# Layer 2 of the 448-token slots with the weights stationary, and the way back of its rows through DRAM

## The chip, the core and the metric

The kernel runs on one core of a Trainium2 chip. The time is the device time of one execution in microseconds (us). The five engines of the core that matter here are TensorE (PE; PEld is its weight load), VectorE (DVE), ScalarE (ACT), GpSimd (POOL) and SyncE (SP), which issues most of the DMAs. Every engine works through its own instructions in order.

## The reference

The tokens pass through an attention with sigmoid weights; then each of the 3584 tokens goes to one of eight experts, whose two layers are a matmul, a ReLU and a matmul.

```
x = attn_out.transpose(0, 2, 1, 3).reshape(3584, 768)
e_idx = np.argmax(x @ w_gate, axis=1)
gate_w = softmax(x @ w_gate)[e_idx]
eom = 1.0 / (1.0 + np.exp(-(x @ w_output_gate)))
for e in range(8):
    mask = e_idx == e
    h = np.maximum(x[mask] @ w1[e], 0.0)      # 768 -> 1024
    ye = h @ w2[e]                            # 1024 -> 768
    out[mask] = gate_w[mask, None] * eom[mask, e, None] * ye
```

## The kernel before

The first part is the attention, which also writes x to DRAM (`x_dram`) and routes the tokens: for each expert a list of its tokens' rows. The second part works in slots. A slot is up to 448 tokens of one expert (a 448-token slot, `TB`) or up to 240 (a half slot, `TM`). With these inputs nine slots run: seven of 448 tokens and then two half slots. The first four 448-token slots always run; those after them and the half slots stand in branches.

All matmuls of a slot are done as three, because each operand is split into a high part and a low part (`split`: ACT copies the rounded high part, DVE subtracts to get the low part): high times high, low times high, high times low.

Layer 1 of a slot has eight groups f of 128 hidden units. A group is 6 x 3 matmuls (L458 to L460) with w1 stationary and the tokens moving, 448 or 240 columns. ACT then writes the ReLU's high part (L471, `hh`) and DVE its low part (L472, `hl`; for a 448-token slot in two pieces, 384 and 64 columns, since the low part of the last 64 tokens lies next to their high part in `hr`).

Layer 2 before has the tokens stationary: for 128 tokens t and one half n of the 768 outputs, 8 x 3 matmuls (L486 to L488) of 384 columns, with the token block as the weights and w2 moving. A 448-token slot has three such blocks and 64 tokens over. Those go through `layer2_rest` (L530, L531): a stationary block of which 64 rows are the high and 64 the low part of the same tokens, 2 x 16 matmuls of 384 columns more. ACT evicts each PSUM tile with the token's weight as scale (L492), and GpSimd scatters the 128 rows to `out` with an indirect DMA (L515). The last PSUM tile of a 448-token slot is kept (`left`) and evicted and scattered in the next slot (`finish`, L506). In a half slot the last 128 rows are scattered in two halves of the columns.

Around the matmuls a slot prepares the next one (`slot`). In layer 1 GpSimd gathers the next slot's x rows (L384, 14 gathers for 448 tokens, 8 for a half slot), w2 of this slot is split in pairs of rows (f = 1 to 4), and SP loads the next w1 in three parts behind it (`w1r` and `w2r` lie in the same memory). After layer 1 DVE transposes the gathered rows (`turn_x`, L428); they are split (`split_x`) and w1 is split (`split_w1`) during layer 2, and SP loads the next w2 in four parts behind that. Layer 2 uses three PSUM banks in turn (`psy`), layer 1 three others (`psh`). The order on each engine is the order in which the code is written (`manual_schedule`). L385 to L397 issue the weight loads; L661 is the attention's store of x, four DMAs of 32 x 14 runs of 192 numbers each.

Of the kernel before, what the change touches and what calls it, by code (L numbers as in the profile page):

```python
# [8 lines left out]
F32 = mybir.dt.float32  # L9
# [12 lines left out]
E = 8  # L22
# [33 lines left out]
class Kernel:  # L56
# [19 lines left out]
    def memory(self):  # L76
        self.rounded = self.pool("rounded").tile([128, ROUNDED // 4], F32R, name="rounded")
        self.plain = self.pool("plain").tile([128, PLAIN // 4], F32, name="plain")
        ps = self.pool("psum", space=PSUM).tile([128, 8, 512], F32, name="ps")
        self.ps_s = [ps[:, 0:2], ps[:, 2:4]]  # L80
        self.ps_o = [[ps[:, 4], ps[:, 5]], [ps[:, 6], ps[:, 7]]]
        self.ps_s2 = ps[:, 6:8]
        self.psh = [ps[:, i] for i in (0, 1, 2)]
        self.psy = [ps[:, i] for i in (4, 5, 3)]
        self.ps_step = [ps[:, i, 0:8] for i in (7, 3)]
        self.rot = {}
        self.beat = [None, None]
        self.hints = {2: [ET.Activation, ET.DVE, ET.Pool], 5: [ET.PE]}

        c = self.carve  # L90
        w = c(0, 3, 2, 2, DF)
        self.w1s = [[w[:, d // 2, a, d % 2] for d in range(6)] for a in range(2)]
        self.w1p = [[w[:, k, a] for k in range(3)] for a in range(2)]
        self.xs = [c(12 * DF * 4 + i * 6 * TB * 4, 6, TB) for i in range(2)]

        self.w1r = c(0, 6, DF, dt=F32)
        self.w2r = c(0, 8, DM, dt=F32)
        self.xg = c(6 * DF * 4, GB_, Q4, dt=F32)
        self.xT = c(6 * DF * 4 + XG, 6, TB, dt=F32)
# [27 lines left out]
    def constants(self):  # L127
# [3 lines left out]
        self.x_dram = dram.tile([NT, DM], F32, name="x_dram")  # L131
        self.lst = dram.tile([E * CAP, W], I32, name="lst")
# [29 lines left out]
        self.halves = cp.tile([128, 3], I32, name="halves")  # L162
        self.left, self.left_at = None, cp.tile([128, 1], I32, name="leftat")
        self.left_w = cp.tile([128, 1], F32, name="leftw")
# [299 lines left out]
    def layer1(self, f, n, begun=False):  # L464
        nc = self.nc
        if not begun:
            self.layer1_mm(f, n)
        ps, r = self.h_ps, n % 128 if n == TB else 0
        m = n - r
        hh, hl, hr = self.hs[0][:, f, 0:n], self.hs[1][:, f, 0:m], self.hr[:, f, r:]  # L470
        self.beat[0] = nc.scalar.activation(hh, ps, AF.Relu).ins  # L471
        lo = lambda out, a, b: nc.vector.scalar_tensor_tensor(  # L472
            out, ps[:, a:b], 0.0, r32(hh[:, a:b]), ALU.max, ALU.subtract)
        lo(hl, 0, m)
        if r:
            lo(hr, m, n)

    def layer2(self, s, t, n, y, last=0):
# [10 lines left out]
        if last == TB and n == 1:  # L489
            self.left = ps  # L490
# [19 lines left out]
    def half_rows(self, at):  # L510
        for n in range(2):
            self.nc.vector.tensor_scalar(self.halves[:, n:n + 1], at, 2.0, float(n), ALU.mult, ALU.add)
# [7 lines left out]
    def layer2_rest(self, s):  # L520
        nc = self.nc
        lt, y = s["lt"], self.ys[1]
        lo, hi = slice(0, 64), slice(64, 128)
        for n in range(2):
            c = slice(384 * n, 384 * n + 384)
            ps = self.take("y", self.psy)[:, 0:384]
            for f in range(8):
                h = self.hr[:, f]
                wh, wl = self.w2_at(f, c)
                nc.tensor.matmul(ps, h, wh, start=(f == 0), stop=False)  # L530
                nc.tensor.matmul(ps, h, wl, start=False, stop=(f == 7))  # L531
            nc.scalar.activation(y[lo, c], ps[hi], AF.Copy, scale=r32(lt[hi, 3, 1:2]))
            nc.vector.scalar_tensor_tensor(y[lo, c], ps[lo], r32(lt[lo, 3, 1:2]), y[lo, c], ALU.mult, ALU.add)
        self.scatter(lt[lo, 3, 0:1], y[lo])

    def slot(self, cur, nxt, side=None, begun=False, hint=None):
# [5 lines left out]
        self.finish()  # L542
        self.rot["y"] = 1
        for f in range(8):
# [20 lines left out]
        ws = {0: (0, 1), 1: (2,)} if n == TB else {0: (0,), 1: (1, 2)}  # L565
        xs = {2: (0,), 3: (1, 2)} if n == TB else {0: (0,), 1: (1,), 2: (2,)}
        for i in range(2 * (n // 128)):
            t = i // 2
            if hint is not None and i in self.hints:
                hinted = self.hints[i]  # L570
                more = self.nc.values_load(self.more[0:1, hint[1]:hint[1] + 1], engines=hinted, min_val=0, max_val=1)
                self.tc.mark_branch_hint_location(hint[0], hint=more, engines=hinted)
            self.layer2(cur, t, i % 2, self.ys[(t + (t > 0 and n % 128 > 0)) % 2], n if t == n // 128 - 1 else 0)
            if nx is not None:
# [4 lines left out]
                for k in xs.get(i, ()):  # L579
                    self.split_x(nx, k)  # L580
            if i == 3 and n == TB:
                self.nc.vector.tensor_copy(self.left_at, cur["lt"][:, 2, 0:1])
                self.nc.vector.tensor_copy(self.left_w, r32(cur["lt"][:, 2, 1:2]))
            if i == 0 and n < TB:
                self.half_rows(cur["lt"][:, 1, 0:1])
            if side is not None:
                next(side, None)
            if i == 1 and n % 128:
                self.layer2_rest(cur)
        return nx  # L590

# [189 lines left out]
    def build(self, phases="abc"):  # L781
# [64 lines left out]
        with tc.manual_schedule():  # L846
            self.finish()
        mid = lambda k: lambda: (self.slot_regs(self.tab_b, k, self.ltb[:, k], self.lxb[:, k], False), NT, False)
        lists = lambda k: dict(lt=self.ltb[:, k], lx=self.lxb[:, k])
        with ExitStack() as ctx:  # L850
            for k in range(E):
                ctx.enter_context(tc.If(part > k))
                with tc.manual_schedule():
                    self.slot(lists(k), mid(k + 1) if k + 1 < E else None)
# [35 lines left out]
```

## Time and profile before

| | |
|---|---|
| median of three runs | 763.12 us (762.82 to 763.97) |
| the profiled execution | 765.36 us |
| its span, first to last instruction | 763.6 us |
| PE busy | 754.4 us, 99% of the span |
| granted TensorE clock | 0.998 |
| DMA | 126.53 MB, mean 166 GB/s |

The profile is of one execution. Times in its rows count from the start of the span. A matmul's row has the time from its start to the end of its pipeline, and the next matmul starts before that; so the pace of PE is read from the distance of the starts. What ended an engine's idle time before an instruction stands behind it as "<-".

### The profile page before, as it was taken

Reading aid. Unit: us, or ns where it says so; the run is one execution under the profiler, and the core shown is the slowest. Engines: PE = TensorE matmul, PEld = TensorE weight load, DVE = VectorE, ACT = ScalarE, POOL = GpSimd, SP = SyncE. Lnnn points to the kernel's source line nnn. Section 1 sums busy time; section 2 is a strip of 40 time slices with the busy share of each in tenths; the row PEclk is TensorE's granted clock in tenths of the full one; section 3 lists DMA queues with packets and bytes.
Section 4 is the critical chain, followed back from the end, with each engine's and each line's share of the span. In section 5 each row is a group of like instructions: output and inputs, shape, how many; then the busy total and the mean of one; then the engine's idle time right before and its main releaser. Section 6 shows DMA issues by size and latency. Waiting matters only on the chain. (4 is left out here: it accounts for less than half of the span.)

```text
span 763.6 us, 14912 instructions
## 1 busy us (share of the span) xinstructions
PE 754.4 (99%) x5817; PEld 580.2 (76%) x5817; DVE 397.9 (52%) x731; ACT 372.0 (49%) x429; POOL 270.7 (35%) x379
## 2 busy tenths in 40 slices
PE   9999999999999999999999999999999999999996
PEld 4444444444344379999999999999999999999996
DVE  1364746556687759524615625615524534454554
ACT  5666666666677632523433424424424433344544
POOL 5002102020444437288237137227217216324142
PEclk9999999999999999999999999999999999999999
DMA  8465665746796646626526425334344352463641
GB/s 302 145 179 145 196 154 162 211 130 172 253 291 194 165 117 207 200 65 210 182 83 221 141 109 194 118 155 160 123 172 127 134 215 85 175 220 111 221 144 41
DMA packets 73721, 126.53 MB, mean 166 GB/s; under 512 B 15442, under 2 KB 53484, under 8 KB 73632
## 3 DMA queue, kind: packets, MB, share of 16 engines
q1 hardware_dynamic: 62784, 99.95, 42.4%
q0 software_dynamic: 9776, 24.53, 9.4%
q10 hardware_dynamic: 1072, 0.92, 0.5%
q8 instruction: 50, 0.82, 0.5%
q14 instruction: 39, 0.32, 0.1%
HBM read 108.77 MB, written 23.09 MB: 173 GB/s over the span
## 5 line engine op out<-in xcount | busy, mean ns | idle before, releaser
L635 ACT ACTIVATE a<-ps,bias_s 128x896 f32<-128x896 f32 x168 | 168.7, 1007 | 86.9 <-PE ps L633 83.6
L384 POOL DMA_INDIRECT plain<-x_dram,lxs x112 | 139.3, 1244 | 76.0 <-ACT h L471 25.2
L633 PE MATMUL ps<-q,k 64*64 64x448 f32 x1344 | 157.9, 541 | 1.2 <-ACT a L635 0.8
L642 PE MATMUL ps<-a,v 64*64 64x448 f32 x1344 | 156.3, 536 | 0.0
L458 PE MATMUL ps<-rounded 128*128 128x448 f32 (+1 forms) x432 | 149.9, 347 | 0.8 <-ACT y L506 0.8
L460 PE MATMUL ps<-rounded 128*128 128x448 f32 (+1 forms) x432 | 149.1, 345 | 0.0
L459 PE MATMUL ps<-rounded 128*128 128x448 f32 (+1 forms) x432 | 149.1, 345 | 0.0
L410 DVE TENSOR_TENSOR rounded<-plain,rounded 128x2048 fp32r<-128x2048 f32 (+5 forms) x63 | 96.8, 1573 | 71.8 <-ACT rounded L409 71.8
L486 PE MATMUL ps<-w2h,h 128*128 128x384 f32 x400 | 133.7, 334 | 0.0
L488 PE MATMUL ps<-w2h,h 128*128 128x384 f32 x400 | 133.7, 334 | 0.0
L487 PE MATMUL ps<-w2l,h 128*128 128x384 f32 x400 | 133.7, 334 | 0.0
L472 DVE SCALAR_TENSOR_TENSOR h<-ps,h 128x384 fp32r<-128x384 f32 (+2 forms) x128 | 44.9, 387 | 139.8 <-ACT h L471 136.7
L471 ACT ACTIVATE h<-ps 128x448 fp32r<-128x448 f32 (+1 forms) x72 | 36.5, 507 | 155.4 <-PE ps L460 148.9
L633 PEld LDWEIGHTS ps<-q,k 64*64 64x64 f32 x1344 | 50.9, 134 | 76.5 <-issue 69.4
L642 PEld LDWEIGHTS ps<-a,v 64*64 64x64 f32 x1344 | 51.6, 133 | 74.7 <-issue 71.3
L458 PEld LDWEIGHTS ps<-rounded 128*128 128x128 f32 x432 | 81.2, 188 | 6.7 <-ACT y L506 1.1
L460 PEld LDWEIGHTS ps<-rounded 128*128 128x128 f32 x432 | 81.2, 188 | 5.0
L459 PEld LDWEIGHTS ps<-rounded 128*128 128x128 f32 x432 | 81.2, 188 | 4.9
L409 ACT CAST rounded<-plain 128x2048 fp32r<-128x2048 f32 (+5 forms) x63 | 81.8, 1331 | 0.6 <-DVE plain L434 0.6
L515 POOL DMA_INDIRECT out<-y,lts x21 | 30.9, 1470 | 136.2 <-ACT y L492 73.3
L487 PEld LDWEIGHTS ps<-w2l,h 128*128 128x128 f32 x400 | 75.1, 188 | 0.1
L486 PEld LDWEIGHTS ps<-w2h,h 128*128 128x128 f32 x400 | 75.1, 188 | 0.1
(146 smaller groups left out, 685.6 us busy)
## 6 DMA issues: line engine op xcount, KB each, us to landing
plain<-w SPq DMA_DIRECT2D x40, 768.0 KB
plain<-w SPq DMA_DIRECT2D x27, 1024.0 KB
k<-kT SPq DMA_DIRECT2D x23, 448.0 KB
q<-qT SPq DMA_DIRECT2D x23, 448.0 KB
x_dram<-xt SPq DMA_DIRECT2D x30, 336.0 KB
v<-vm SPq DMA_DIRECT2D x23, 384.0 KB
plain<-w SPq DMA_DIRECT2D x6, 512.0 KB
plain<-x_dram,lxs POOLq DMA_INDIRECT x112
```

The source lines that it names most:

```text
L384: self.paced(self.nc.gpsimd.indirect_dma_start(out=self.xg[:, g], out_offset=None, in_=x4, in_offset=bass.IndirectOffsetOnAxis(ap=s["lx"][ ...
L409: self.nc.scalar.copy(hi, raw)
L410: self.nc.vector.tensor_tensor(lo, raw, r32(hi), ALU.subtract)
L458: nc.tensor.matmul(ps, wh[d][:, c], xh[:, d, 0:n], start=(d == 0), stop=False)
L459: nc.tensor.matmul(ps, wh[d][:, c], xl[:, d, 0:n], start=False, stop=False)
L460: mm = nc.tensor.matmul(ps, wl[d][:, c], xh[:, d, 0:n], start=False, stop=(d == 5))
L486: nc.tensor.matmul(ps, hh[:, f, tk], wh, start=(f == 0), stop=False)
L487: nc.tensor.matmul(ps, hh[:, f, tk], wl, start=False, stop=False)
L488: nc.tensor.matmul(ps, hl[:, f, tk], wh, start=False, stop=(f == 7))
L633: qk = nc.tensor.matmul(ps[half[h], j, 0:S], k[half[j], e, o:o + 64], q[half[j], e], start=True, stop=True)
L635: self.beat[0] = nc.scalar.activation(at[u % 3], ps[:, :, 0:S], AF.Sigmoid, bias=self.bias_s, scale=1.0 / math.sqrt(D)).ins
L642: nc.tensor.matmul(self.ps_o[e][h][half[j], 0:S], v[half[h], e, c, j], a[half[h], j], start=(i in ((0, 3 if h else 4)[e],)), stop=(i == (2 ...
```

## The change

Layer 2 of the 448-token slots is turned round: w2 is stationary and the tokens move. For each 128 columns c of the output, 8 x 3 matmuls of 448 columns fill one PSUM tile, with 128 output columns on the partitions and 448 tokens in the free dimension (`layer2_turned`); `layer2_rest` is gone. A PSUM tile holds columns now where rows are wanted. DVE transposes it in blocks of 32 x 32 into `yq` (`turn_back`), which lies where `xT` lies, so that `split_x` of the next slot comes first. For the rows to come out in order, w2 is split into an order of columns in which each 128 holds four runs of 32, one of each quarter of the row (`split_w2`, now one row f at a time).

The sixth tile is turned in the next slot, and `finish` is a generator that moves the rows on in steps: at the start of the next slot's layer 1 eight DMAs store `yq` to `y_dram`; after its layer 1 two blocks of 128 rows are loaded back; in its layer 2 ACT scales them by the tokens' weights in place and GpSimd scatters them, then the other two blocks (128 and 64 rows) follow in the same two buffers. After the last 448-token slot the same is done in the first half slot, at f = 4, at f = 6 and after layer 1. Half slots keep their layer 2, with one scatter of whole rows at the end in place of two of half rows, and an eviction that puts the columns back in order.

```
+        self.yq = c(6 * DF * 4 + XG, GB_, Q4, dt=F32)
...
-        self.hs = [self.h2[:, :, 0:TB], self.h2[:, :, TB + TB % 128:]]
-        self.hr = self.h2[:, :, TB - TB % 128:TB + TB % 128]
+        self.hs = [self.h2[:, :, 0:TB], self.h2[:, :, TB:2 * TB]]
...
+        self.y_dram = dram.tile([TB, DM], F32, name="y_dram")
...
     def split_w2(self, k):
-        rows = lambda w: w[k // 3][:, 2 * k % 6:2 * k % 6 + 2]
-        self.split(self.w2r[:, 2 * k:2 * k + 2], rows(self.w2h), rows(self.w2l))
+        for f in (2 * k, 2 * k + 1):
+            h, l = (w[f // 6][:, f % 6].rearrange("p (c a x) -> p a c x", a=4, x=32) for w in (self.w2h, self.w2l))
+            self.split(self.w2r[:, f].rearrange("p (a c x) -> p a c x", a=4, x=32), h, l)
...
+    def layer2_turned(self, c):
+        nc = self.nc
+        hh, hl = self.hs
+        ps = self.take("y", self.psy)[:, 0:TB]
+        for f in range(8):
+            wh, wl = self.w2_at(f, slice(128 * c, 128 * c + 128))
+            nc.tensor.matmul(ps, wh, hh[:, f], start=(f == 0), stop=False)
+            nc.tensor.matmul(ps, wl, hh[:, f], start=False, stop=False)
+            nc.tensor.matmul(ps, wh, hl[:, f], start=False, stop=(f == 7))
+        return ps
+
+    def turn_back(self, ps, c):
+        self.nc.vector.transpose(self.yq[:, :, 32 * c:32 * c + 32], ps.rearrange("p (g t) -> p g t", t=32))
...
-        nc.scalar.activation(y[:, c], ps, AF.Copy, scale=r32(s["lt"][:, t, 1:2]))
-        if 0 < last < TB:
-            i = self.scatter(self.halves[:, n:n + 1], y[:, c], 2)
-            if n:
-                self.tc.declare_no_dep(i, self.first_half, reason="the other half of each row")
-            else:
-                self.first_half = i
-                nc.gpsimd.memset(self.halves[0:1, 2:3], 0)
-        elif n == 1:
-            self.scatter(s["lt"][:, t, 0:1], y)
-
-    def finish(self):
-        if self.left is not None:
-            y = self.ys[1]
-            self.nc.scalar.activation(y[:, 384:768], self.left, AF.Copy, scale=self.left_w)
-            self.scatter(self.left_at, y)
-            self.left = None
+        nc.scalar.activation(y.rearrange("p (a c x) -> p c a x", a=4, x=32)[:, 3 * n:3 * n + 3],
+                             ps.rearrange("p (c a x) -> p c a x", a=4, x=32), AF.Copy, scale=r32(s["lt"][:, t, 1:2]))
+        if n == 1:
+            self.scatter(s["lt"][:, t, 0:1], y)
+
+    def finish(self, ys):
+        if self.left is None:
             return
+        nc = self.nc
+        self.turn_back(self.left, 5)
+        rows = self.y_dram.rearrange("(g t) (a x) -> a t g x", t=32, a=4)
+        for g in (slice(0, 8), slice(8, GB_)):
+            for a in range(4):
+                nc.sync.dma_start(rows[a, :, g], self.yq[32 * a:32 * a + 32, g])
+        yield
+        for two in ((0, 1), (2, 3)):
+            parts = [(t, slice(0, 128 if t < 3 else 64)) for t in two]
+            for t, r in parts:
+                nc.sync.dma_start(ys[t % 2][r], self.y_dram[128 * t:128 * t + r.stop])
+            yield
+            for t, r in parts:
+                y = ys[t % 2][r]
+                nc.scalar.activation(y, y, AF.Copy, scale=self.left_w[r, t:t + 1])
+                self.scatter(self.left_at[r, t:t + 1], y)
+            if two[0]:
+                yield
...
     def slot(self, cur, nxt, side=None, begun=False, hint=None):
...
-        self.finish()
+        fin = self.finish(self.ys if n == TB else (self.hb, self.ys[1]))
+        next(fin, None)
         self.rot["y"] = 1
...
+            if f in (4, 6) and n < TB:
+                next(fin, None)
...
         for k in range(3):
             self.turn_x(nx, k)
-        ws = {0: (0, 1), 1: (2,)} if n == TB else {0: (0,), 1: (1, 2)}
-        xs = {2: (0,), 3: (1, 2)} if n == TB else {0: (0,), 1: (1,), 2: (2,)}
-        for i in range(2 * (n // 128)):
+        if n == TB:
+            next(fin, None)
+            self.layer2_columns(cur, nx, side, hint, fin)
+            return nx
+        next(fin, None)
+        ws = {0: (0,), 1: (1, 2)}
+        for i in range(4):
             t = i // 2
...
+    def layer2_columns(self, cur, nx, side, hint, fin):
+        for k in range(3):
+            self.split_x(nx, k)
+        for c in range(6):
...
+            ps = self.layer2_turned(c)
+            if nx is not None and c < 3:
+                self.split_w1(c)
+                for j in range(c, 4 if c == 2 else c + 1):
+                    self.load_w2(nx, j)
+            if c < 5:
+                self.turn_back(ps, c)
+            if c in (0, 2):
+                next(fin, None)
+            if c == 5:
+                lt = cur["lt"]
+                self.nc.vector.tensor_copy(self.left_at, lt[:, :, 0])
+                self.nc.vector.tensor_copy(self.left_w, r32(lt[:, :, 1]))
+            if side is not None:
+                next(side, None)
+        self.left = ps
```

How the order of instructions moves is shown at three places.

The first is DVE in layer 2 of a late 448-token slot. Before, behind the transposes of x (L428) the low parts of w1 come (L410, 128x2048), then those of x (128x896), and nothing of them has to do with the PSUM tiles but L533.

```order
L428 STREAM_TRANSPOSE plain<-plain 128x14x2x32 [waits DVE_49] x2
L410 TENSOR_TENSOR rounded<-plain,rounded 128x2048 [waits DMAHW7_49,PE_49,Activation_49]
L410 TENSOR_TENSOR rounded<-plain,rounded 128x2048 [waits DMAHW0_49,PE_49,Activation_49]
L410 TENSOR_TENSOR rounded<-plain,rounded 128x2048 [waits DMAHW1_49,PE_49,Activation_49]
L533 SCALAR_TENSOR_TENSOR y_2662<-ps,lts,y_2662 64x384 [waits Activation_49] x2
```

Now the low parts of x come first, and the transposes out of PSUM (L486) stand between and behind those of w1.

```order
L429 STREAM_TRANSPOSE plain<-plain 128x14x2x32
L410 TENSOR_TENSOR rounded<-plain,rounded 128x896 [waits PE_49,Activation_49] x3
L410 TENSOR_TENSOR rounded<-plain,rounded 128x2048 [waits DMAHW2_49,Activation_49]
L486 STREAM_TRANSPOSE plain<-ps 128x14x32 [waits DVE_49,PE_49]
L410 TENSOR_TENSOR rounded<-plain,rounded 128x2048 [waits DMAHW3_49,Activation_49]
L486 STREAM_TRANSPOSE plain<-ps 128x14x32 [waits PE_49]
```

The first PSUM tile is released by the seventh DVE instruction behind the last transpose of x or a half of it, where ACT released it before.

The second place is ACT in the first half slot, from f = 5 on. Before, the ReLUs (L471) are followed by the evictions of layer 2 (L492) with the splits of the next slot's w1 and x (L409) between them.

```order
L471 ACTIVATE h<-ps 128x240 [waits PE_49,Activation_49] x3
L492 ACTIVATE y_2661<-ps,ltb 128x384 [waits DMASW2_49,DMASW0_49,DMASW4_49,PE_49,DMASW6_49,Activation_49,Pool_49]
L409 CAST rounded<-plain 128x2048 [waits DMAHW7_49]
L409 CAST rounded<-plain 128x2x256 [waits DVE_49,Activation_49]
L492 ACTIVATE y_2661<-ps,ltb 128x384 [waits PE_49,Activation_49]
L409 CAST rounded<-plain 128x2048 [waits DMAHW0_49]
L409 CAST rounded<-plain 128x2048 [waits DMAHW1_49]
L409 CAST rounded<-plain 128x2x256 [waits DVE_49,Activation_49]
```

Now two scalings (L521) stand ahead of the last ReLU and two ahead of the first eviction (L499), each behind a load (DMAHW); `hb` and `y_2662` are the buffers.

```order
L471 ACTIVATE h<-ps 128x240 [waits PE_49,Activation_49] x2
L521 ACTIVATE hb<-hb,leftw 128x768 [waits DMAHW5_49,DVE_49,Pool_49]
L521 ACTIVATE y_2662<-y_2662,leftw 128x768 [waits DMASW5_49,DMASW7_49,DMASW3_49,DMAHW6_49,DMASW1_49,Activation_49]
L471 ACTIVATE h<-ps 128x240 [waits PE_49]
L521 ACTIVATE hb<-hb,leftw 128x768 [waits DMAHW0_49]
L521 ACTIVATE y_2662<-y_2662,leftw 64x768 [waits DMAHW1_49,DMASW0_49,Activation_49]
L499 ACTIVATE y_2661<-ps,ltb 128x3x4x32 [waits DMASW4_49,DMASW6_49,DMASW2_49,PE_49]
L409 CAST rounded<-plain 128x2048 [waits DMAHW3_49]
```

The four scalings moved into the half slot's ACT order in front of work that was there.

The third place is GpSimd in the same half slot, from the seventh gather on. Before, the gathers (L384) follow each other, and the scatters (L515) come in layer 2.

```order
L384 DMA plain<-x_dram,lxb 128x192 [waits DMASW2_49,PE_49]
L384 DMA plain<-x_dram,lxb 128x192 [waits DMASW3_49,PE_49]
L515 DMA out<-y_2661,ltb 3584x768 [waits DMASW4_49,Activation_49,Pool_49]
L515 DMA out<-y_2662,halves 7168x384 [waits DMASW4_49,DMASW5_49,DVE_49,Activation_49]
L499 MEMSET halves 1x1
```

Now two scatters (L527) stand ahead of the last gather. GpSimd's DMAs take eight semaphores in turn (DMASW0 to 7), and each waits for its own from eight DMAs ago.

```order
L384 DMA plain<-x_dram,lxb 128x192 [waits DMASW6_49,PE_49]
L527 DMA out<-hb,leftat 3584x768 [waits DMASW7_49,Activation_49]
L527 DMA out<-y_2662,leftat 3584x768 [waits DMASW7_49,DMASW0_49,Activation_49]
L384 DMA plain<-x_dram,lxb 128x192 [waits DMASW1_49,PE_49]
L527 DMA out<-hb,leftat 3584x768 [waits DMASW2_49,DMASW0_49,Activation_49]
L527 DMA out<-y_2662,leftat 3584x768 [waits DMASW3_49,DMASW2_49,Activation_49]
```

Each scatter also names the semaphore of the scatter ahead of it (the second that of the first, DMASW7; the third that of the second, DMASW0), so they follow each other's landing.

## Rows read from the trace of the kernel before

**Rows 1.** The page's head and part 1: busy time, share, instructions.
```profile
span 763.6 us, 14912 instructions
PE 754.4 (99%) x5817; PEld 580.2 (76%) x5817; DVE 397.9 (52%) x731; ACT 372.0 (49%) x429; POOL 270.7 (35%) x379
```

**Rows 2.** Stretches: us, sum, busy PE, PEld, DVE, ACT, POOL, PEclk, DMA share, GB/s.
```profile
630.80:691.00 60.20, 60.02 (x323) 57.56 (x322) 26.68 (x33) 22.36 (x26) 23.93 (x18) 1.00 0.45 153
691.00:725.00 34.00, 33.34 (x245) 33.38 (x246) 20.18 (x23) 17.91 (x23) 11.81 (x11) 1.00 0.52 181
```

**Rows 3.** Matmuls in order of time, slot 4: layer 1, layer 2, next slot.
```profile
451.52 0.37 PE L459 MATMUL ps<-rounded 128*128 128x448 f32 x1
...
480.50 0.34 PE L486 MATMUL ps<-w2h,h 128*128 128x384 f32 x1
...
511.04 0.21 PE L450 MATMUL ps<-zero 128*128 128x8 bf16 x2
```

**Rows 4.** Groups of instructions, shapes kept apart: busy, mean ns | idle.
```profile
L410 DVE TENSOR_TENSOR w2l<-plain,w2h 128x1536 fp32r<-128x1536 f32 x36 | 63.4, 1761 | 18.3 <-ACT w2h L409 15.5 <-issue 2.7
...
L656 DVE STREAM_TRANSPOSE xt<-x 128x448 f32<-128x448 f32 x48 | 31.0, 645 | 1.6
...
L410 DVE TENSOR_TENSOR rounded<-plain,rounded 128x768 fp32r<-128x768 f32 x1 | 1.0, 959 | 0.9 <-ACT rounded L409 0.9
...
L409 ACT CAST rounded<-plain 128x768 fp32r<-128x768 f32 x1 | 0.8, 833 | 0.6 <-DVE plain L434 0.6
```

**Rows 5.** DVE in order of time, layer 2 of slot 4.
```profile
481.89 3.09 DVE L428 STREAM_TRANSPOSE plain<-plain 128x896 f32<-128x896 f32 x3
487.35 6.70 DVE L410 TENSOR_TENSOR rounded<-plain,rounded 128x2048 fp32r<-128x2048 f32 x3 [2.38 <-ACT rounded L409]
```

**Rows 6.** SP's DMA issues: a store of x, loads in slot 4.
```profile
40.34 3.88 SPq L661 DMA_DIRECT2D x_dram<-xt  x4
...
466.19 28.98 SPq L395 DMA_DIRECT2D plain<-w  x7
```

**Rows 7.** SP's issues in the first half slot, and the DMA then.
```profile
701.64 22.84 SPq L395 DMA_DIRECT2D plain<-w  x7
...
702.65:711.50 8.85, 8.85 (x69) 8.85 (x69) 4.09 (x6) 2.28 (x4) 3.25 (x3) 1.00 0.98 370
```

**Rows 8.** First half slot: its first matmul and the next slot's.
```profile
691.65 0.35 PE L458 MATMUL ps<-rounded 128*128 128x240 f32 x1 [0.83 <-ACT y L506]
...
724.51 0.27 PE L458 MATMUL ps<-rounded 128*128 128x240 f32 x1
```

**Rows 9.** First half slot, other engines in order of time.
```profile
708.12 0.37 ACT L471 ACTIVATE h<-ps 128x240 fp32r<-128x240 f32 x1 [1.65 <-PE ps L460]
...
712.83 2.41 ACT L409 CAST rounded<-plain 128x2048 fp32r<-128x2048 f32 x2
...
716.93 4.22 ACT L409 CAST rounded<-plain 128x2048 fp32r<-128x2048 f32 x3
...
707.29 0.94 POOL L384 DMA_INDIRECT plain<-x_dram,lxb  x1 [0.86 <-PE ps L460]
...
713.81 1.90 DVE L428 STREAM_TRANSPOSE plain<-plain 128x512 f32<-128x512 f32 x3 [4.87 <-DMA plain<-x_dram,lxb]
...
718.87 5.70 DVE L410 TENSOR_TENSOR rounded<-plain,rounded 128x2048 fp32r<-128x2048 f32 x4 [0.26 <-ACT rounded L409]
```

**Rows 10.** Chain that ended last: a whole-row scatter, issue to landing.
```profile
750.08 3.25 DMA out<-y,ltb
```

**Rows 11.** PE in order of time at the kernel's start.
```profile
0.95 2.71 PE L716 MATMUL ps<-rounded 128*128 128x256 f32 x11 [0.95 <-DVE bias_s L698]
3.92 3.56 PE L633 MATMUL ps<-q,k 64*64 64x448 f32 x24 [0.25 <-DMA k<-kT]
7.29 0.94 PE L642 MATMUL ps<-a,v 64*64 64x448 f32 x8
8.04 0.94 PE L633 MATMUL ps<-q,k 64*64 64x448 f32 x8
```

More of the change, by code (lines that the diff above doesn't have):

```diff
@@ L161, in constants @@
         nc.gpsimd.memset(self.zero, 0.0)
-        self.halves = cp.tile([128, 3], I32, name="halves")
-        self.left, self.left_at = None, cp.tile([128, 1], I32, name="leftat")
-        self.left_w = cp.tile([128, 1], F32, name="leftw")
+        self.left, self.left_at = None, cp.tile([128, 4], I32, name="leftat")
+        self.left_w = cp.tile([128, 4], F32, name="leftw")
         self.eps = cp.tile([64, NB], F32, name="eps")
@@ L467, in layer1, with layer2 @@
             self.layer1_mm(f, n)
-        ps, r = self.h_ps, n % 128 if n == TB else 0
-        m = n - r
-        hh, hl, hr = self.hs[0][:, f, 0:n], self.hs[1][:, f, 0:m], self.hr[:, f, r:]
+        ps = self.h_ps
+        hh, hl = (h[:, f, 0:n] for h in self.hs)
         self.beat[0] = nc.scalar.activation(hh, ps, AF.Relu).ins
[L472 to L478, printed above, removed]
+        nc.vector.scalar_tensor_tensor(hl, ps, 0.0, r32(hh), ALU.max, ALU.subtract)
+    def layer2_turned(self, c):
[10 more added lines that the diff above has]
+        self.nc.vector.transpose(self.yq[:, :, 32 * c:32 * c + 32], ps.rearrange("p (g t) -> p g t", t=32))
+    def layer2(self, s, t, n, y):
         nc = self.nc
@@ L518, in scatter @@
             in_=y, in_offset=None, bounds_check=parts * NT - 1, oob_is_err=False).ins
[L520 to L534, printed above, removed]
     def slot(self, cur, nxt, side=None, begun=False, hint=None):
@@ L564, in slot @@
             self.turn_x(nx, k)
-        ws = {0: (0, 1), 1: (2,)} if n == TB else {0: (0,), 1: (1, 2)}
-        xs = {2: (0,), 3: (1, 2)} if n == TB else {0: (0,), 1: (1,), 2: (2,)}
-        for i in range(2 * (n // 128)):
-            t = i // 2
[L569 to L573, printed above, removed]
+        if n == TB:
[5 more added lines that the diff above has]
+        for i in range(4):
+            t = i // 2
+            self.layer2(cur, t, i % 2, self.ys[t])
             if nx is not None:
@@ L578, in slot @@
                         self.load_w2(nx, j)
[L579 to L585, printed above, removed]
+                if i < 3:
+                    self.split_x(nx, i)
             if side is not None:
                 next(side, None)
-            if i == 1 and n % 128:
-                self.layer2_rest(cur)
-        return nx
+        return nx
+    def layer2_columns(self, cur, nx, side, hint, fin):
+        for k in range(3):
+            self.split_x(nx, k)
+        for c in range(6):
+            if hint is not None and c in self.hints:
+                hinted = self.hints[c]
+                more = self.nc.values_load(self.more[0:1, hint[1]:hint[1] + 1], engines=hinted, min_val=0, max_val=1)
+                self.tc.mark_branch_hint_location(hint[0], hint=more, engines=hinted)
+            ps = self.layer2_turned(c)
[14 more added lines that the diff above has]
+        self.left = ps
     def attention(self, pool):
@@ L845, in build @@
                     cur = self.slot(cur, late(k + 1), hint=(f"big{k + 1}", k + 1) if k + 1 < LATE_MAX else None)
-        with tc.manual_schedule():
-            self.finish()
         mid = lambda k: lambda: (self.slot_regs(self.tab_b, k, self.ltb[:, k], self.lxb[:, k], False), NT, False)
         lists = lambda k: dict(lt=self.ltb[:, k], lx=self.lxb[:, k])
[L850 to L854, printed above, removed]
+        half = lambda k: self.slot(lists(k), mid(k + 1) if k + 1 < E else None)
+        with tc.If(part > 0) as some:
+            with tc.manual_schedule():
+                half(0)
+            left, self.left = self.left, None
+            with ExitStack() as ctx:
+                for k in range(1, E):
+                    ctx.enter_context(tc.If(part > k))
+                    with tc.manual_schedule():
+                        half(k)
+            self.left = left
+        with some.Else():
+            with tc.manual_schedule():
+                for _ in self.finish(self.ys):
+                    pass
 @with_exitstack
```

5 lines of the change are left out of this document (removed).

## The prediction

> **What bounds the kernel now.** The page's head and its busy times come first: PE works 754.4 of 763.6 us and DVE, ACT and GpSimd half of the span or less [rows 1]. So the time is the sum of what PE issues, plus the few places where it waits. The profiled execution took 765.36 us, 1.76 more than its span; the sums below go against 765.36, and 2.24 comes off for the median of 763.12.
>
> The busy times by stretch show the same inside the slots: of 60.2 us of the last 448-token slot PE has 60.0, DVE 26.7, ACT 22.4, GpSimd 23.9, and the DMA moves 153 GB/s; in the first half slot they are 33.3, 20.2, 17.9 and 11.8 of 34.0 [rows 2]. The matmuls in order of time give PE's pace: layer 1 of slot 4 is 144 matmuls of 448 columns, and from the second to the first of layer 2 are 480.50 - 451.52 = 28.98 us, so 0.2027 us each; layer 2 is 144 matmuls and the 32 of `layer2_rest`, all of 384 columns, in 30.54 us up to the two small ones that begin the next slot, so 0.1735 each [rows 3].
>
> **The change part by part.** *Layer 2 on PE.* 144 matmuls of 448 columns by 0.2027 are 29.2 us where there were 30.5: 1.36 us less, in seven slots **-9.5 us**. Layer 1 has this form already (weights stationary, 448 columns moving), so its pace is the nearest row; weight loads stay as many per matmul.
>
> *DVE and ACT in the 448-token slots.* Six transposes of 128x448 are added; the attention has such at 0.645 us, out of SBUF [rows 4], together 3.9. The splits of w2 come in twice as many pieces: two of 128x768 for one of 128x1536 is 2 x 0.959 - 1.761 = 0.16 on DVE, four times 0.6 [rows 4]. ACT gains four scalings near 0.83 (a 128x768 cast) and loses eight evictions of 0.58 [rows 4, 9]. DVE stays under 32 of 58.5 us and ACT near 22; even if the runs of 32 numbers doubled every split they would stay under PE. Cost nothing; without this cover, at most the 3.9 of the transposes would show.
>
> *When the banks come free.* A PSUM bank is now released by DVE, and three are used in turn, so PE's fourth column group needs the first bank 3 x 24 x 0.2027 = 14.6 us into layer 2. DVE's order is x's three transposes, three low parts of x, one of w1, then `turn_back`. In slot 4 the transposes began 1.4 us into layer 2 and took 3.1 [rows 5]; low parts of 128x896 are some 1.1 each by the 0.959 of 768, that of w1 2.2 (6.70 for three), the transpose 0.65 [rows 4, 5]. That ends 10.5 to 11 us into layer 2: about 3.6 us to spare, taken as no stall.
>
> *SP and DMA.* The store of `yq` is 1792 runs of 192 numbers, as many as the attention's store of x, whose four DMAs were issued in 3.88 us; here there are eight, so 3.9 to 7.8 [rows 6]. SP's next work is w1 at 466.19, some 15 us into slot 4 [rows 6], in the half slot at 701.64, 10 us into it [rows 7, 8]: hidden. The loads of blocks 2 and 3 make SP wait for the scatters, and the last three loads of w2 stand behind that, wanted only by the splits of the next slot: hidden. Store and loads are 2 x 1.38 MB more per slot, 46 GB/s more over 60 us: some 200 where 370 was moved with the DMA full [rows 2, 7].
>
> *The first half slot* takes the rows of the last 448-token slot, and here the cover ends. T0 is its first matmul, 691.65 [rows 8]. Before, the last low part of x for the next half slot (the fourth DVE piece from 718.87) ends at 724.57, T0 + 32.9 [rows 9], and PE starts that slot at 724.51 [rows 8]; so there is hardly any slack, and ACT, which casts ahead of DVE, stands right ahead of it. Now ACT has four scalings in that queue, each behind a load (second order view):
> - the loads of blocks 0 and 1 stand behind w1 loads on SP, issued from 701.64, with data from 702.65 at a full 370 GB/s [rows 7]. Two w1 parts of 1.05 MB are 5.7 us, a block of 0.39 MB another 1.1: T0 + 18.0 and 19.1. Scaled by 19.9. The ReLU of f = 7, at T0 + 16.5 before [rows 9], stands behind both; PE wants it as the eighth f of layer 2, 16.1 + 21 x 0.1735 = T0 + 19.7. About 0.6 us of waiting, most of it inside what follows.
> - scatter 0 goes out at T0 + 18.9. A whole-row scatter with the DMA idle took 3.25 from issue to landing [rows 10]; a gather under the loads went out at 707.29 and DVE waited for it until 713.81, 6.5 us [rows 9]. I take 4.0, nearer the idle end since the w1 loads are done by 711.5: T0 + 22.9. Scatter 1 waits for that landing: 26.2.
> - block 3 is loaded once scatter 1 has left its buffer: 1.0 from issue to first data [rows 7], 0.5 for the rest: 27.8. Scaled: 28.6.
> - only then come the evictions (0.58) and casts (2.41 for two, 4.22 for three) [rows 9]: ACT ends the casts up to x's second pair at 28.6 + 0.58 + 2.41 + 0.58 + 4.22 = 36.4. DVE's low parts, 2.2 for w1 and 0.6 for x, follow at their own pace and end at T0 + 39.1.
>
> PE wants that low part after the six matmuls of d = 0 and 1 of the next slot, 724.51 + 0.67, T0 + 33.5: **+5.6 us**. Bounds: with every scatter at 3.25 and no queueing ahead of blocks 0 and 1 the chain is 3.9 shorter, +1.7; with both scatters at 6.5 it is 5.7 longer, +11.3.
>
> [...]
>
> *The end.* The last half slot scatters whole rows where half rows were last: 197 KB more behind the last eviction, at 370 GB/s **+0.5 us** (bounds 0 and the 0.94 of one more issue of a gather's kind [rows 9]). PE's pause at the change to the half slot, 0.83 for ACT [rows 8], should stay: DVE's last `turn_back` takes ACT's place.
>
> **Sum:** -9.5 + 5.6 + 0.5 = -3.4; 765.4 gives 762.0, the median **759.7 us**. The bounds of the half slot alone give 755.8 to 765.4.
>
> **The rivals.** *The half slot's chain is mostly hidden.* If blocks 0 and 1 slip in ahead of the w1 data and the scatters land in 3.25, the loss is 1.7 to 3.5: 755.8 to 757.6. For it: the DMA is idle after 711.5. Against it: the order of SP's queue. Chance 0.14.
>
> *The clock falls in the wait.* In the sum PE stands some 4.5 us almost still around T0 + 34.6 to 39.1 (two waits of 1.8 and 2.6). Nowhere in the trace does PE rest that long; at the start, after rest, eleven matmuls of 256 columns took 2.71 us, 0.246 each, and 24 of the attention 3.37 where the next eight took 0.75 [rows 11]: against 0.114 (the 0.2027 scaled to 256 columns) and 0.094 this is 1.4 + 1.1 = 2.5 us lost; the mean granted clock of 0.998 leaves room for 1.5 us of that by the clock. If the same comes here: 762.2. The pauses under 1 us at slot changes left the pace as it was, and the two waits are nearer to those, so the sum holds nothing for it. [...] Chance 0.2.
>
> *The half slot's chain is long.* Both scatters near 6.5, since store, loads and gathers share their queues: a loss of 8 to 11.3, 762.1 to 765.4. Against it: the w1 loads are over. Chance 0.14.
>
> *The 448-token slots stall* (the other side). If the y loads, issued at the end of layer 1, delay the last gathers, x's transposes begin late and hold DVE, and PE waits for the bank at c = 3 in every slot. From 3.6 us of delay each further us costs 7 us: slower than before from 3.6 + 4.9/7 = 4.3 us, transposes at 5.7 us into layer 2 instead of 1.4; one us more, 766.7. For it: under loads a gather took 6.5 us. Against it: the DMA's mean stays near 200 GB/s. Chance 0.12.
>
> **How the numbers follow.** The forecast, a loss of 5 to 8 in the half slot, has 0.4: 757.5 to 762. With the rivals, 0.2% of 763.12 (1.5 us, about what a measurement can tell from no change) puts the borders at 761.6 and 764.6. Faster: 0.36 of the forecast, 0.14 of the hidden chain, 0.08 of the clock: 0.58. Same: 0.04, 0.12 of the clock, 0.05 of the long chain: 0.21. Slower: the rest of the long chain 0.09 and the stalls 0.12: 0.21. The range reaches to 755 and 766; that leaves out the worst of stalls and a chain better than every bound.
>
> **What the profile after would show.** Layer 2 of a 448-token slot: 29.2 us from its first matmul to the next slot, without a wait for DVE at the fourth group; transposes out of PSUM near 0.65; the store hidden. In the first half slot: ACT idle for loads ahead of the last ReLU and again until about T0 + 28, the second scatter behind the first's landing, and PE waiting some 5 us at the start of the second half slot, with matmuls at 0.11 behind it (at twice that, the clock). Wrong would be the prediction if PE waits in the 448-token slots for PSUM banks, if layer 2's matmuls lie over 0.203 apart, or if that wait in the half slot is under 3.5 or over 8 us.

## The result and the profile after

The changed kernel takes 774.55 us (774.13 to 775.78) against 763.39 before: a ratio of 1.0149, 95% interval 1.0131 to 1.0166. Slower by 11 us where 3.4 less were forecast. The page of the profile after begins as follows (compare [rows 1]).

```profile
span 772.4 us, 14526 instructions
PE 748.9 (97%) x5593; PEld 558.6 (72%) x5593; DVE 413.1 (53%) x735; ACT 370.7 (48%) x437; POOL 235.5 (30%) x375
```

PE has 5.5 us less to do and the span is 8.8 longer, so PE stands still where it did not. The view of waits on PE says for what (total, times, longest):

```profile
PE ps L459 <- DVEq L858: 7.8, 1, 7.8
PE ps L460 <- DVE rounded L410: 2.6, 2, 2.4
PE ps L496 <- ACT y L499: 1.8, 1, 1.8
PE ps L496 <- ACT h L471: 1.5, 1, 1.5
PE ps L459 <- ACT rounded L409: 1.4, 1, 1.4
```

L858 is the branch that ends the 448-token slots. The largest wait by far is a single one, at the change to the half slots; the others lie in the half slots. Next the busy time by stretch, with the columns of [rows 2]: the fifth and seventh 448-token slots, the change, and the first half slot's start in two pieces.

```profile
503.93:562.44 58.51, 58.51 (x291) 54.07 (x291) 28.85 (x33) 21.97 (x26) 18.67 (x18) 1.00 0.62 202
620.95:679.26 58.31, 58.31 (x290) 54.05 (x290) 28.67 (x33) 21.97 (x26) 18.66 (x18) 1.00 0.63 210
679.26:687.38 8.12, 0.36 (x2) 0.03 (x1) 0.24 (x2) 0.00 (x0) 0.92 (x1) 0.78 0.39 150
687.38:691.20 3.82, 3.82 (x20) 3.82 (x21) 0.65 (x1) 0.00 (x0) 0.74 (x1) 0.56 0.34 71
691.20:701.30 10.10, 10.10 (x93) 10.10 (x92) 7.59 (x12) 7.76 (x13) 4.80 (x6) 1.00 0.85 223
```

The 448-token slots are what was forecast, full of PE at 58.5 us. In the change PE does nothing for 8 us, and in the 3.8 us behind it the mean granted clock is 0.56 and 20 matmuls run where over 30 would (93 in the next 10.1 us). DVE in that stretch shows what is late:

```profile
684.11 0.17 DVE L603 COPY leftat<-lts 128x4 int32<-128x4 int32 x1 [8.65 <-DMA out<-y,leftat]
684.18 0.16 DVE L604 COPY leftw<-lts 128x4 f32<-128x4 f32 x1
688.23 0.65 DVE L486 STREAM_TRANSPOSE plain<-ps 128x448 f32<-128x448 f32 x1 [3.89 <-DVEq L858]
```

At the end of a 448-token slot DVE copies the slot's lists to `leftat` and `leftw`. The scatters of the slot before still read `leftat` as their row numbers, so the copy has to wait for the last of them to land, 684.11. Only then does DVE come to the branch, and PE begins 3 us later.

Where the difference of the two spans lies, by the starts of matmuls:

| part | before | after | change |
|---|---|---|---|
| attention, up to the first pair of small matmuls | 275.20 | 272.37 | -2.83 |
| seven 448-token slots, to the last matmul | 415.28 | 406.89 | -8.39 |
| last matmul to the first half slot's first | 1.17 | 8.12 | +6.95 |
| two half slots, to the last matmul | 65.46 | 77.48 | +12.02 |
| last matmul to the end | 6.49 | 7.54 | +1.05 |
| span | 763.6 | 772.4 | +8.80 |

The attention's code is unchanged, and its end varies from 272.4 to 275.4 over the profiles here, so its -2.83 is not the change's.

### The profile page after: what moved, and what is told of

The parts are those of the page before. It is cut to its first block, busy times and chain, and to the rows that moved or that the text cites. A ratio compares the mean times of both kernels' runs of the same rounds, so it can differ in the third digit from the quotient of the medians.

```text
span 772.4 us, 14526 instructions
## 1 busy us (share of the span) xinstructions
PE 748.9 (97%) x5593; PEld 558.6 (72%) x5593; DVE 413.1 (53%) x735; ACT 370.7 (48%) x437; POOL 235.5 (30%) x375
## 5 line engine op out<-in xcount | busy, mean ns | idle before, releaser
L459 PE MATMUL ps<-rounded 128*128 128x448 f32 (+1 forms) x432 | 151.6, 351 | 9.1 <-DVEq L858 7.8
L460 PE MATMUL ps<-rounded 128*128 128x448 f32 (+1 forms) x432 | 150.9, 349 | 2.6 <-DVE rounded L410 2.6
L461 PE MATMUL ps<-rounded 128*128 128x448 f32 (+1 forms) x432 | 150.6, 349 | 0.0
L384 POOL DMA_INDIRECT plain<-x_dram,lxs x112 | 110.9, 990 | 109.6 <-ACT h L471 61.9
L471 ACT ACTIVATE h<-ps 128x448 fp32r<-128x448 f32 (+1 forms) x72 | 36.5, 507 | 207.8 <-PE ps L461 207.7
L481 PE MATMUL ps<-h,w2l 128*128 128x448 f32 x336 | 122.9, 366 | 0.0
L480 PE MATMUL ps<-h,w2h 128*128 128x448 f32 x336 | 122.8, 366 | 0.0
L482 PE MATMUL ps<-h,w2h 128*128 128x448 f32 x336 | 122.8, 366 | 0.0
L410 DVE TENSOR_TENSOR rounded<-plain,rounded 128x2048 fp32r<-128x2048 f32 (+5 forms) x63 | 96.1, 1565 | 13.4 <-ACT rounded L409 13.4
L472 DVE SCALAR_TENSOR_TENSOR h<-ps,h 128x448 fp32r<-128x448 f32 (+1 forms) x72 | 41.3, 573 | 107.3 <-ACT h L471 107.2
L459 PEld LDWEIGHTS ps<-rounded 128*128 128x128 f32 x432 | 82.7, 191 | 15.4 <-issue 8.8
L409 ACT CAST rounded<-plain 128x2048 fp32r<-128x2048 f32 (+5 forms) x63 | 81.8, 1332 | 20.5 <-DVE plain L429 19.2
L460 PEld LDWEIGHTS ps<-rounded 128*128 128x128 f32 x432 | 82.8, 192 | 8.1 <-DVE rounded L410 3.0
L461 PEld LDWEIGHTS ps<-rounded 128*128 128x128 f32 x432 | 82.7, 191 | 5.2
L527 POOL DMA_INDIRECT out<-y,leftat x26 | 32.2, 1239 | 160.3 <-issue 69.8
L410 DVE TENSOR_TENSOR w2l<-plain,w2h 128x768 fp32r<-128x768 f32 x72 | 65.9, 956 | 3.1 <-ACT w2h L409 0.7
L481 PEld LDWEIGHTS ps<-h,w2l 128*128 128x128 f32 x336 | 63.1, 188 | 5.2
```

What stands on the lines that cost most here:

```text
L384: self.paced(self.nc.gpsimd.indirect_dma_start(out=self.xg[:, g], out_offset=None, in_=x4, in_offset=bass.IndirectOffsetOnAxis(ap=s["lx"][ ...
L409: self.nc.scalar.copy(hi, raw)
L410: self.nc.vector.tensor_tensor(lo, raw, r32(hi), ALU.subtract)
L459: nc.tensor.matmul(ps, wh[d][:, c], xh[:, d, 0:n], start=(d == 0), stop=False)
L460: nc.tensor.matmul(ps, wh[d][:, c], xl[:, d, 0:n], start=False, stop=False)
L461: mm = nc.tensor.matmul(ps, wl[d][:, c], xh[:, d, 0:n], start=False, stop=(d == 5))
```

## The experiments

The kernel before was timed beside each; its median lay between 763.3 and 765.5 us, so the ratios are what is compared.

**1. The lists staged (e1_staged_lists).** The wait for `leftat` is taken away by a second pair of tiles.

```
+        self.next_at, self.next_w = cp.tile([128, 4], I32, name="nextat"), cp.tile([128, 4], F32, name="nextw")
...
-                self.nc.vector.tensor_copy(self.left_at, lt[:, :, 0])
-                self.nc.vector.tensor_copy(self.left_w, r32(lt[:, :, 1]))
+                self.nc.vector.tensor_copy(self.next_at, lt[:, :, 0])
+                self.nc.vector.tensor_copy(self.next_w, r32(lt[:, :, 1]))
...
         yield
+        nc.vector.tensor_copy(self.left_at, self.next_at)
+        nc.vector.tensor_copy(self.left_w, self.next_w)
         for two in ((0, 1), (2, 3)):
```

> DVE copies the last slot's lists into a stage at the end of layer 2 and from there to the scatters' lists only in the next slot, so the copy at the end of a slot no longer waits for a scatter's landing. Theory (the wait of 8.65 us for that landing holds DVE, and all engines meet at the change to the half slots): PE's gap there falls from 8.1 to about 1.2 us, no half-speed matmuls behind it (1.6 us less), 774.5 - 6.9 - 1.6 = 766 us. Rival (the gap comes from the new branch around the half slots): gap and time stay, 774.5.

Measured: 770.79, ratio 1.0075 (1.0057 to 1.0093). PE in order of time, at the change and at the half slots' two longest waits:

```profile
680.67 0.35 PE L460 MATMUL ps<-rounded 128*128 128x240 f32 x1 [0.85 <-DVEq L861]
...
705.58 0.69 PE L497 MATMUL ps<-w2h,h 128*128 128x384 f32 x1 [4.89 <-ACT h L472]
...
726.15 0.57 PE L461 MATMUL ps<-rounded 128*128 128x240 f32 x1 [2.45 <-DVE rounded L411]
```

The gap is 1.21 us instead of 8.12, with the new branch still there, so the copy's wait made it and the rival falls. The time came down by 0.74% (5.7 us), not 8.5: the half slots take 80.42 us in this profile and 77.48 in that of the changed kernel. The wait for the last ReLU grew from 1.5 to 4.9: PE, without the slow matmuls at its start, asks for it 1.6 us sooner behind the half slot's first matmul, and block 0 of the rows (tokens 0 to 127 of the last 448-token slot) comes 1.8 us later behind it, 22.7 instead of 20.9. Behind the waits at the second half slot 29 matmuls run at half speed (0.21 us apart, granted clock 0.50 from 728 to 732) instead of 17. The seven slots now take 405.7 us from the first small matmuls to the last matmul, 9.55 less than before.

**2. The half slot without the way back (e3_half_bare).**

```
-        fin = self.finish(self.ys if n == TB else (self.hb, self.ys[1]))
+        fin = self.finish(self.ys) if n == TB else iter(())
```

> As e1, but the first half slot leaves out the way back of the last 448-token slot's rows (the sixth transpose, store, loads, scalings, scatters: those rows are not written). What the half slots cost without it: 755 us by the theory, which puts all loss behind 687 us on that way back; over 760 if the half slots lose time for another reason (their eviction into strided columns, w2 in other order).

Measured: 756.83, ratio 0.9883 (0.9866 to 0.9899); PE waits nowhere in the half slots, which take 65.42 us from the first to the last matmul (before 65.46). All that is lost behind the change hangs on these row blocks: their eviction into strided columns and w2's order of columns cost nothing that shows. This is also the bound of what the turned layer 2 can give here.

**3. The scalings moved (e2_half_order, and e4_order_only without the staged lists).** The first two scalings and scatters go behind f = 7, the second two behind ACT's casts.

```
-            if f in (4, 6) and n < TB:
+            if f in (4, 7) and n < TB:
...
-        next(fin, None)
         ws = {0: (0,), 1: (1, 2)}
...
-                if i < 3:
-                    self.split_x(nx, i)
+                for k in {0: (0,), 1: (1, 2)}.get(i, ()):
+                    self.split_x(nx, k)
+            if i == 1:
+                next(fin, None)
```

> As e1, and in the half slot the first two scalings and scatters come after the ReLU and the gather of f = 7, the second two after the casts for the next slot's w1 and x. Theory (the wait at the second half slot comes from ACT's and GpSimd's queues behind the scatters, with the clock's fall as its consequence): no wait over 0.5 us in the half slots and no half-speed matmuls at 731; against e1 some 8.2 us of waits and 2 of clock less: 756 us. Rival (the moved bytes of rows themselves, on DMA and SP, delay the second half slot): 762 to 766.

> The changed kernel with only the reordering of e2 in the half slot, lists as they were. Theory (two separate causes that add up): the gap of 8.1 us with the slow matmuls behind it stays, the waits at 710 to 731 go: 774.5 - 10 = 764 us. Rival (the late start of the half slot is what makes its chain late): waits stay, 772 to 774.

Measured: e2 774.13, ratio 1.0114 (1.0097 to 1.0131); e4 780.18, 1.0183 (1.0166 to 1.02). Both are slower than without the move, which neither theory nor rival had. In e2 the waits ahead of the second half slot go and 1.41 us of those at its start is left, but a new one of 13.71 us comes inside it, for a PSUM bank that ACT and DVE free late. ACT and GpSimd there:

```profile
718.83 0.94 ACT L524 ACTIVATE y<-y,leftw 64x768 f32<-64x768 f32 x1 [3.82 <-DMA y<-y_dram]
733.94 1.05 ACT L500 ACTIVATE y<-ps,ltb 128x384 f32<-128x384 f32 x2 [14.17 <-DMA out<-y,leftat]
...
716.46 1.45 POOL L530 DMA_INDIRECT out<-y,ltb  x1 [4.73 <-DMA out<-y,leftat]
725.61 0.98 POOL L530 DMA_INDIRECT out<-hb,leftat  x1 [7.70 <-issue]
730.91 0.92 POOL L530 DMA_INDIRECT out<-y,leftat  x1 [4.31 <-issue]
```

The eviction at 733.94 writes the buffer out of which the fourth block is scattered. That scatter stands in GpSimd's row behind three others, each of which waits for the one ahead to land; beside the loads of w2, that took 9.2 and 5.3 us from issue to issue. So the scatters in series are a cause of their own, and moved work meets them. e4 shows a gap of 7.36 us at the change beside a wait of 15.97 (in the profile of an execution of 784.9 us): the two causes are separate.

**4. One link of the chain at a time (e6_early_loads, e7_scatters_apart).** e6 is e1 with `if f in (1, 6)`; e7 is e1 with this:

```
-                self.scatter(self.left_at[r, t:t + 1], y)
+                i = self.scatter(self.left_at[r, t:t + 1], y)
+                if t % 2 and len(ys) == 2 and ys[0] is self.hb:
+                    self.tc.declare_no_dep(i, first, reason="other rows")
+                first = i
```

> As e1 with one edit: the first two blocks are loaded at f = 1 of the half slot instead of f = 4, so ahead of w1 on SP and on the DMA. Theory (the wait of 4.9 us for the ReLU of f = 7 is the loads' queueing behind w1): that wait goes; the second pair of scalings still stands ahead of the casts but ends some 6 us earlier, so the waits of the second half slot stay near 4 to 5 us; ratio 1.0075 less 5 us, 1.001. Rival (the scatters set the chain): the chain ends as late as in e1, waits at the second half slot grow by what f = 7 gives back, ratio 1.006 or more.

> As e1, with the second scatter of each pair in the half slot not ordered behind the first (they write other rows). Theory (each landing of some 3.5 us is in the chain): the third block's load of the half slot is issued 3 to 4 us earlier for the fourth block, the second half slot's waits shrink by 2 to 3.5 us; ratio 1.0035. Rival (the loads behind w1 alone set it): no change, 1.0075.

Measured: e6 765.68, ratio 1.0034 (1.0023 to 1.0045); e7 764.67, 1.0022 (1.0011 to 1.0034). In e6 the wait for the last ReLU is gone, as expected, but 5.4 us come back as PE's wait for a bank that the first eviction has to free, which stands behind the second scalings; the result lies between theory and rival. e7 is about 4 us faster than e1, as the theory had it, but in its profile less than half of that is the shorter chain. Block 3's load was issued 2.7 us earlier (1.3 behind block 2's instead of 4.0), and the waits at the second half slot came down from 4.2 to 2.5 us. The rest is the pace of the matmuls behind these waits, which came 0.21 us apart in e1. PE in e7 waits there once instead of twice, and the matmuls behind it keep their distance of 0.11 us:

```profile
720.47 0.27 PE L460 MATMUL ps<-rounded 128*128 128x240 f32 x1
723.12 0.38 PE L461 MATMUL ps<-rounded 128*128 128x240 f32 x1 [2.38 <-DVE rounded L411]
...
723.45 0.28 PE L460 MATMUL ps<-rounded 128*128 128x240 f32 x1
723.57 0.28 PE L461 MATMUL ps<-rounded 128*128 128x240 f32 x1
```

The 29 half-speed matmuls that e1 has at this place, some 2.9 us, are gone; in all the half slots take 75.4 us instead of 80.4.

**5. Buffers of their own, and scatters that do not wait for each other (e5_own_buffers, e8_free_scatters).** e5 uses free memory for a third block, loads three ahead of w1 and scales them after f = 7:

```
+        own = self.xg.rearrange("p g e -> p (g e)")[:, 8 * Q4:8 * Q4 + DM]
+        fin = self.finish(self.ys if n == TB else (self.hb, self.ys[1], own))
...
+            if f in (1, 7) and n < TB:
```

with the casts as in e2, so that only the fourth block, in `hb` again, comes behind them. e8 adds that each scatter of the half slots is declared independent of the earlier ones (they write other rows).

> As e1, but in the first half slot three blocks have a buffer each (the third in the free end of the gathered rows' memory) and are loaded at f = 1, ahead of the w1 loads; they are scaled and scattered after the ReLU and gather of f = 7, the fourth block is loaded behind the first's or second's scatter and scaled after the casts for the next slot. Theory (the loss in the half slots is the row blocks' late loads and their scalings in front of ACT's casts): PE waits under 1 us in the half slots, ratio to before 0.989 to 0.992, within 2 us of the bare half slot (0.9883). Rival (the row transfers cost the half slots their weight loads' time, wherever they stand): PE waits 2 us or more for casts of w1, ratio over 0.993.

> As e5, and no scatter of the half slots is ordered behind another (they all write other rows). Theory (what is left of the loss in e5 is GpSimd's queue: each scatter waits for the landing of the one ahead, the second half slot's gathers come late behind them, x is turned late, and ACT's last evictions stand behind its casts): the gathers of the second half slot follow PE again, the last eviction comes within 1 us of PE's last matmul, ratio to before 0.990 (0.988 to 0.992, the bare half slot had 0.9883). Rival (the late gathers come from the loads on the DMA): ratio stays near 1.000.

Measured: e5 764.66, ratio 1.0012 (0.9997 to 1.0028). PE's waits there are as the theory had them, 0.9 us in the half slots, and still the kernel is no faster than the one before. The loss has moved to the end, which is 16.5 us long from PE's last matmul (746.83) on, against 7.3 in e3. GpSimd and ACT show it:

```profile
731.10 0.92 POOL L530 DMA_INDIRECT out<-hb,leftat  x1 [3.62 <-ACT h L472]
...
744.92 0.95 POOL L385 DMA_INDIRECT plain<-x_dram,lxb  x1 [0.30 <-PE ps L498]
...
755.77 2.12 POOL L530 DMA_INDIRECT out<-y,ltb  x1 [2.86 <-ACTq L875]
...
748.74 0.62 ACT L410 CAST rounded<-plain 128x512 fp32r<-128x512 f32 x1 [11.59 <-DVE plain L430]
...
754.36 1.04 ACT L500 ACTIVATE y<-ps,ltb 128x384 f32<-128x384 f32 x2
```

The scatters in series hold GpSimd, so the second half slot's last gather goes out at 744.92 and its x is turned late; the cast of that x holds ACT for 11.59 us with the last evictions behind it, and the last scatter starts 9 us after PE is done. (That x is for a third half slot, which these inputs do not have.) e8: 757.88, ratio 0.9909 (0.9893 to 0.9926), faster than both kernels. GpSimd in the second half slot:

```profile
717.36 0.92 POOL L536 DMA_INDIRECT out<-hb,leftat  x1 [0.30 <-ACT y L500]
718.58 0.98 POOL L536 DMA_INDIRECT out<-y,ltb  x1 [0.30 <-issue]
...
731.73 0.94 POOL L385 DMA_INDIRECT plain<-x_dram,lxb  x1 [1.00 <-PE ps L462]
...
750.11 1.00 POOL L536 DMA_INDIRECT out<-y,ltb  x1 [7.16 <-ACT y L500]
```

The scatters follow each other without a pause, the last gather comes 13 us earlier, and the last scatter 1.3 us after PE's last matmul (748.81). The rival, loads on the DMA, falls. What is left against the bare half slot is 0.26%, some 2 us.

## Why the prediction was wrong, point by point

**Layer 2 on PE: right.** 1.36 us less per slot were forecast, with a layer 2 of 29.2; that of the fifth slot took 29.18 (533.26 to 562.44). The slots from the third to the sixth are 58.51 us from small matmuls to small matmuls, where before 59.87 lie between them; the first is 1.35 shorter. The second, though, took 59.66 in the changed kernel and in e4, and 58.5 in all seven kernels with staged lists (for instance e1, 328.59 to 387.12): a pace of 0.207 instead of 0.203 through the whole slot, without a wait of PE and at a granted clock of 1.00. Why stays open; with staged lists the seven slots gained 9.55 against 9.5 forecast.

**Banks, DVE, ACT, SP, DMA: right.** DVE in layer 2 of the fifth slot, which begins at 533.26 (compare [rows 5]):

```profile
534.77 3.10 DVE L429 STREAM_TRANSPOSE plain<-plain 128x896 f32<-128x896 f32 x3
537.79 5.26 DVE L410 TENSOR_TENSOR rounded<-plain,rounded 128x896 fp32r<-128x896 f32 x4
542.96 0.64 DVE L486 STREAM_TRANSPOSE plain<-ps 128x448 f32<-128x448 f32 x1
```

The first bank is free 10.3 us into layer 2, of the 14.6 that PE leaves (10.5 to 11 forecast). DVE has 28.7 to 28.9 us per slot and the DMA 202 to 210 GB/s. The store took SP 5.44 us in the half slot (3.9 to 7.8).

**The change to the half slot: this step failed.** "PE's pause at the change to the half slot, 0.83 for ACT [rows 8], should stay: DVE's last `turn_back` takes ACT's place." It went from 1.17 to 8.12. I counted DVE's transposes and left out the two list copies, though the diff shows them. Before, they had one column and stood at the fourth PSUM tile, long after the scatter that read the list; now they are the last DVE work of a slot, and the scatter that reads the list is the fourth of the slot, itself behind three landings. From the second slot to the sixth DVE waited like this too (37 us in total), without a wait of PE, since DVE's next work in layer 1 had room; at the branch PE waited 7.8 us, to 3.0 us behind DVE's last instruction. e1 shows this by itself.

**The half slot's chain: mechanism right, size wrong.** Forecast 5.6, measured 12.0, with PE's waits as named and one more, 1.8 us for the first eviction, which stands behind the second scalings. ACT, then GpSimd, then SP in the first half slot, T0 = 687.38:

```profile
708.32 0.94 ACT L521 ACTIVATE hb<-hb,leftw 128x768 f32<-128x768 f32 x1 [4.54 <-DMA hb<-y_dram]
...
715.71 0.94 ACT L521 ACTIVATE hb<-hb,leftw 128x768 f32<-128x768 f32 x1 [5.23 <-DMA hb<-y_dram]
720.13 0.93 ACT L521 ACTIVATE y<-y,leftw 64x768 f32<-64x768 f32 x1 [3.48 <-DMA y<-y_dram]
...
709.53 1.02 POOL L527 DMA_INDIRECT out<-hb,leftat  x1 [6.01 <-ACT hb L521]
713.49 1.00 POOL L527 DMA_INDIRECT out<-y,leftat  x1 [2.94 <-DMA out<-hb,leftat]
...
697.59 3.32 SPq L395 DMA_DIRECT2D plain<-w  x2
701.05 0.37 SPq L517 DMA_DIRECT2D hb<-y_dram  x1
...
716.97 0.48 SPq L517 DMA_DIRECT2D y<-y_dram  x1
```

Block 0 was there at T0 + 20.9 instead of 18.0 (whose own terms, 11.0 + 5.7 + 1.1, add up to 17.8). The slow matmuls at the start had no part in it: SP began on the w1 loads at T0 + 10.2, before at T0 + 10.0. From 697.59 to 708.32 the DMA moved 3.6 MB at 339 GB/s, where I had counted 2.5 MB (two parts of w1 and the block) at 370; so other transfers went beside the block. In e6, which loads it ahead of w1, it was there at T0 + 15.9. The scatters were sized well: scatter 0 went out at 709.53 and scatter 1 at 713.49, 4.0 later as taken; block 3's load was issued at 716.97, 3.5 later (3.25). The load of block 3 was not: 3.2 us from issue to scaling where 1.0 + 0.5 stood, since I took the first data and the bytes and nothing behind them: its bytes moved from 718.2 to 719.2, and ACT began 0.9 us after the last. ACT ends at T0 + 33.7 instead of 28.6, and PE's last wait at T0 + 43.9 instead of 39.1. Adding these 4.8 and the 1.7 of slow matmuls behind the last wait turns the forecast 5.6 into 12.1. PE's waits alone come to 8.3, which lies in the range of the rival "the half slot's chain is long" (8 to 11.3), but not by its cause: that was two scatters near 6.5 us, and they took 4.0 and 3.5.

**The clock: the rival was right.** PE in order of time in the second half slot's first group, and then the busy time by stretch behind it, with the columns of [rows 2]:

```profile
726.86 0.27 PE L461 MATMUL ps<-rounded 128*128 128x240 f32 x1
728.48 0.38 PE L459 MATMUL ps<-rounded 128*128 128x240 f32 x1 [1.35 <-ACT rounded L409]
731.31 0.38 PE L460 MATMUL ps<-rounded 128*128 128x240 f32 x1 [2.45 <-DVE rounded L410]
...
732.23 0.41 PE L459 MATMUL ps<-rounded 128*128 128x240 f32 x1
732.44 0.41 PE L460 MATMUL ps<-rounded 128*128 128x240 f32 x1
```

```profile
732.50:735.00 2.50, 2.50 (x13) 2.50 (x13) 0.41 (x1) 0.37 (x1) 0.00 (x0) 0.50 1.01 404
735.00:745.00 10.00, 10.00 (x90) 10.00 (x90) 7.79 (x12) 7.70 (x13) 8.38 (x6) 1.00 0.48 173
```

After two waits with one matmul between them the distance of the starts is 0.21 instead of 0.11, at a granted clock of 0.50, until about 735; the same came behind the gap of 8 us (0.50 from 687.4 to 690). Behind the two single waits of the first half slot (1.9 and 2.2 us from start to start) the clock stayed at 1.00. In each slow stretch some 16 or 17 matmuls took 0.10 more, 1.6 to 1.7 us, where the rival had put 2.5 from the kernel's start (there the trace of before has a granted clock of 1.00, from 0 to 8 us; its mean of 0.998 comes from 0.82 behind 755). The first stretch lies ahead of the waits and took the place of waiting: in e1, without it, PE waits longer for block 0. I had given the rival 0.2 because the two waits seemed nearer to the pauses at slot changes than to the rest at the start.

**The end:** +1.05 with the whole-row scatter, 0.5 forecast; the bare half slot has 7.28 us there, 0.8 more than before.

So the sum would have been -9.5, +6.95 at the change, +12.0 in the half slots, +1.05: +10.5, and 11.2 were measured; the second slot's 1.15 makes it 11.7. With both causes away (e8) the change is worth 7.5 us.

## What to carry to other kernels

Look in a diff for small writes into buffers that a DMA still reads: here a copy of 128x4 numbers had to wait for the landing of the last scatter that read the list, five times (37 us in total) without a wait of PE, and then for 8.65 us ahead of a branch, where PE waited 7.8. Scatters that write different rows were ordered one behind the other here until the code said that they are independent (e7, e8); each link cost a landing (3.3 to 4.0 us in the changed kernel and e1, 5.3 and 9.2 beside loads in e2) and held GpSimd with all that was queued behind it (e5's last gather went out 13 us later than e8's). And when an experiment removes a wait and the time stays, follow the queues to the end of the kernel: e5 had 0.9 us of PE's waits left in the half slots and lost 9 us after PE's last matmul.

## What the runs showed of the hardware

- At the branch that ends the 448-token slots PE of the changed kernel began 3.0 us after DVE's last instruction (684.34 to 687.38), and DVE's own next one came 3.9 after it. With DVE early, the gap was 1.2 to 1.5 in e1, e3, e5 and e8.
- In the changed kernel the granted clock was 0.50 behind waits of 1.6 and 2.8 us with a single matmul between them and behind the change (8.1 us; all waits from start to start), and matmuls of 240 columns came 0.21 us apart instead of 0.11. Behind single waits of 5.2 us in e1 and 5.8 in e7 matmuls of 384 columns came 0.32 us apart instead of 0.17; the mean granted clock in e1 was 0.79 there (706 to 712). Behind single waits of 1.9 and 2.2 us in the changed kernel the clock stayed at 1.00, and behind one of 2.7 in e7 the distance stayed at 0.11.
- In the changed kernel a row block of 192 KB that SP loaded from DRAM with little else on the DMA (67 GB/s from 716.97 to 720.13, the block among it) was used 3.2 us after its issue, 0.9 after its last bytes moved.
- A uniform slowdown of 2% through one whole slot, in the changed kernel and e4, with no wait in it and at a granted clock of 1.00 in its 59.66 us: unexplained.
